# Linear attention with a GEGLU gate: the residual's x goes to another place, and the order of all engines is planned anew

## The chip, the cores and the metric

The kernel runs on one core of a Trainium2 chip. The metric is the time of one execution on the device in microseconds (us), the median of several runs.

## What is computed

```python
x = A_x                                   # [1, 2048, 512]
xn = layernorm(x)
qkv = xn @ wqkv                           # 32 heads of 16
phi = lambda t: where(t > 0, t + 1, exp(t)) + 1e-6
pq, pk = phi(q), phi(k)
kv = einsum("bhsd,bhse->bhde", pk, v);  z = pk summed over s
o = (pq @ kv) / (pq . z + 1e-6)           # by head
s = o @ wo
g = silu((gelu(xn @ w_gate) * (xn @ w_up)) @ w_down)   # hidden size 1792
out = x + s * g
```

## The kernel before

All data are float32. A matrix product is made of three matmuls on rounded halves: `split` (L494) writes a tile as a high part h (cast on ACT, L486) and a low part l = tile - h (subtraction on DVE, L492), and `sum3` (L498) adds h*h, h*l and l*h into one PSUM tile; the matmuls themselves are L508. On top of that, each 2x2 block product is made of seven products of sums of blocks instead of eight (`PRODUCTS`); X, Y, Z in the names of PSUM tiles are the accumulators of such a group, and the "forms" of an operand are the sums of its blocks that the seven products need, split into h and l.

The tokens are in two halves of 1024: p=1 is the second half, p=0 the first. The stages follow one another, with work of neighbouring stages mixed:

- first stage: layer norm, k, q, and the sum over the tokens; q and the forms of xn go to DRAM (q_d, x_d),
- the FFN of p=1, then of p=0: `quad` (PSUM tiles FX, FY, FZ; then fu and fe, copies of them that ACT makes; g and h on ACT, DVE and POOL) and `down` (DX, DY, DZ, added into acc by DVE, L1099),
- mixed into the FFN of p=0, the queries: a tile q comes back from q_d, POOL makes u = q * zacc, DVE den, its reciprocal rr and q * rr, PE transposes it (ptq, L1165), ACT copies it to pT, and it goes to DRAM (pn_d); `kv_part` loads the tiles wvg0 to wvg3 and PE makes pkv (L1245); `m_part` and its forms ms,
- the last stage, by `s_quad`: its operand's blocks pb come from pn_d and are made into forms, for p=1 in the place Xh and Xl (where the FFN's forms of xn were), for p=0 in sf0 and sf1. The products go to SX, SY, SZ, SV. With the gate g (for p=1 read back from DRAM as g1_0 to g1_7, for p=0 in acc) they are multiplied and added to x, which `x_again` loads once more from in_xt, one tile of 128 x 1024 for each k of 0 to 3: xp10 to xp13 for p=1, xp00 to xp03 for p=0. The sums go to out_y: for p=1 in four stores of 512 KB, for p=0 in nine smaller ones. The su2, su3 and se tiles are copies of SX that ACT makes, since the next product goes into the same SX.

Nothing of this is issued as written. Each operation is recorded by `do` of the class `Plan`, which knows for each its engine, its cost and what it has to wait for; PE's order is partly given by `pe_keys`, and `order` then finds one order for all five engines. `first_order` links the operations with lags (`MARGIN` is added to the lags into PE, into the other engines, and behind a load), schedules them by due times, and then, for each seed in `STEPS`, `nudged` shifts some of the due times at random in one place of the program and the schedule is made again. `MOVES` holds for each kind of DMA the time from issue to transfer, the time behind the transfer, and what is added to it for the engines. All DMAs are issued by SP, in the order found; a DMA whose wait is not over holds up those behind it. The engines, too, do their operations strictly in order.

A place holds one tile after another (`tile_in`): what writes the new tile waits for all readers of the tile before. The tiles xp and pb of the last stage rotate through the nine places of `ring("br", BR)`:

```python
got[k] = tile_in("dp", ring("br", BR), [P, HALF], F32, f"xp{p}{k}", 4)
dma(got[k], ext(xt[k * P:(k + 1) * P, p * HALF:(p + 1) * HALF]), 512, "first")
```

Of the kernel before, what the change touches and what calls it, by code (L numbers as in the profile page):

```python
# [11 lines left out]
F32 = mybir.dt.float32  # L12
# [5 lines left out]
P = 128  # L18
# [61 lines left out]
class Plan:  # L80

    RATE = 400.0
    MOVES = {"load": (0.72, 0.8, 0.0), "first": (0.72, 0.8, 0.7), "store": (0.45, 0.43, 0.0), "pieces": (0.45, 0.43, 0.6)}
    TAIL = {"PE": 0.19, "ACT": 0.13, "DVE": 0.12, "POOL": 0.07, "SP": 0.0}
    HEAD = {"PE": 0.14, "ACT": 0.01, "DVE": 0.01, "POOL": 0.04, "SP": 0.05}
    SAME = {"ACT": 0.15, "DVE": 0.13, "POOL": 0.09}
    BEGIN = 0.65
    ISSUE = 0.85
    ROUNDS = 14
    MARGIN = (0.1, 0.12, 1.0)  # L90
    STEPS = (28, 30, 51, 59, 73, 79, 109, 133, 151, 156, 172, 196, 242, 268, 273, 283, 305, 321, 344, 349, 369, 373, 379, 396, 407, 410, 416, 442, 471, 488, 517, 546, 586, 603, 690, 731, 752, 755, 789, 806, 811, 885, 999, 1028, 1071, 1082, 1197, 1229, 1260, 1313, 1328, 1454, 1461, 1487, 1505, 1523, 1531, 1582, 1598, 1619, 1714, 1744, 1809, 1825, 1884, 1908, 2199, 2256, 2425, 2509, 2559, 2587, 2830, 2905, 3004, 3279, 3386, 3411, 3415, 3433, 3457, 3592, 3702, 3921, 4000, 4006, 4030, 4174, 4182, 4277, 4425, 4583, 4716, 5136, 5149, 5175, 5225, 5401)
    WAIT = 0.3
    FIXED = 4

# [4 lines left out]
    def do(self, eng, cost, fn, out, *ins, more=(), key=None, name="", kb=0, kind="load"):  # L99
# [7 lines left out]
        op.pre, op.suc = set(), []  # L107
        op.way, op.land, gap = self.MOVES[kind]
        op.kb = kb / self.RATE + gap if kb else 0.0
# [204 lines left out]
    def first_order(self, pe_keys):  # L314

        self.link(pe_keys, 0.0, 0.0, 0.0)
        self.plain = self.ahead
        chain = self.link(pe_keys, *self.MARGIN)
        self.wide = self.ahead
# [25 lines left out]
    def order(self, pe_keys):  # L345

        late, done = self.first_order(pe_keys)
        at = self.plan_times(done)
        for seed in self.STEPS:
            late = self.nudged(late, at, seed)  # L350
# [27 lines left out]
def kernel(  # L378
# [17 lines left out]
    KT = D // P  # L396
# [16 lines left out]
    def tile_in(pool_name, unit, shape, dtype, name, parts=1):  # L413

        gen = gens[pool_name, unit] = Gen(gens.get((pool_name, unit)))
        kept = []

        def get():
            if not kept:
                kept.append(pools[pool_name].tile(shape, dtype, name=name, tag=f"{pool_name}{unit}", bufs=1))  # L420
            return kept[0]
        return View([Res() for _ in range(parts)], get, gen, pool_name == "ps")
# [3 lines left out]
    def ring(tag, places):  # L426
        n = count[tag] = count.get(tag, -1) + 1
        return places[n % len(places)]
# [28 lines left out]
    def ext(ap):  # L457
        return View((), lambda: ap)

    def dma(dst, src, kb, kind="load"):  # L460
        do("SP", 0.475, lambda o, i: nc.sync.dma_start(o, i), dst, src, kb=kb, kind=kind, name=kind)
# [857 lines left out]
    BR = [12, 13, 14, 6, 7, 8, 9, 10, 11]  # L1319
    HALF = 2 * NC  # L1320
# [87 lines left out]
    def x_again(p):  # L1408

        got = {}  # L1410
        for k in (0, 2, 1, 3):
            got[k] = tile_in("dp", ring("br", BR), [P, HALF], F32, f"xp{p}{k}", 4)
            dma(got[k], ext(xt[k * P:(k + 1) * P, p * HALF:(p + 1) * HALF]), 512, "first")
        return got

    forms, gg, xps = {}, {}, {}
    for p in (1, 0):
        forms[p] = s_forms(p)
        if p:
            gg[p] = {}  # L1420
            for n, key in enumerate(KEYS):
                gg[p][key] = U("fc" if n < 4 else "fg", FC if n < 4 else FG, f"g1_{n}")
                dma(gg[p][key], g1_d(n, n), 256)
            silus([gg[p][key] for key in KC])
        else:
            gg[p] = {key: acc[0, key] for key in KEYS}
        xps[p] = x_again(p)
        for c in range(2):
            s_quad(p, c, forms[p], gg[p], xps[p])
# [57 lines left out]
```

## Time and profile before

| | |
|---|---|
| median of 3 runs | 612.13 us (611.35 to 613.45) |
| profiled execution | 613.6 us, its span 611.9 us |
| busy PE / DVE / POOL / ACT | 595.7 / 482.1 / 361.6 / 337.8 us |
| granted clock of PE, mean | 0.993 |
| moved by DMA | 145.24 MB, 237 GB/s over the span |

The time is the whole execution, the span reaches from the first to the last instruction that the profiler has; 1.7 us lie around it. Busy times overlap, so they don't add up to the span. Three operations stand for most of what an engine does: a matmul of 128 x 512 (0.39 us from its start to its modelled end, though the next one starts 0.22 to 0.23 us later), an addition on DVE (0.68 us) and a copy or cast on ACT (0.59 to 0.62 us).

### The profile page before, as it was taken

How to read it: one execution, taken by the hardware profiler on the slowest of the kernel's cores; microseconds unless marked ns; L12 is line 12 of the kernel's file. 1: busy time of each engine (PE TensorE's matmuls, PEld its weight loads, DVE VectorE, ACT ScalarE, POOL GpSimd, SP SyncE). 2: the span in 40 equal slices, each digit the busy share in tenths (PEclk: the TensorE clock that was granted, in tenths of full speed). 3: DMA queues.
4: the chain of work that ended last, by engine and by line, in shares of the span. 5: the costliest groups of instructions: out<-in, count | busy, mean ns of one | idle time of the engine just before them, and what ended most of it. 6: DMA issues, size and time to landing. Idle time of an engine off the chain costs nothing. (4 is left out here: it accounts for less than half of the span.)

```text
span 611.9 us, 8235 instructions
## 1 busy us (share of the span) xinstructions
PE 595.7 (97%) x2696; PEld 491.0 (80%) x2696; DVE 482.1 (79%) x698; ACT 337.8 (55%) x611; POOL 361.6 (59%) x300
## 2 busy tenths in 40 slices
PE   8999999999999999999999999999999999989993
PEld 7888888888788888888888888886887888868883
DVE  6989988885798888998888837557557976959995
ACT  6677777875676644663563136453244532558731
POOL 4734754644778877886686126454226751758574
PEclk9999999999999999999999999999999999989998
DMA  7269521359558649764659975987499996788446
GB/s 260 75 225 300 182 76 71 121 172 328 204 202 302 252 151 334 283 221 143 227 220 407 363 299 189 300 284 276 140 319 325 313 346 210 273 293 278 152 139 238
DMA packets 59370, 145.24 MB, mean 237 GB/s; under 512 B 5568, under 2 KB 17088, under 8 KB 59328
## 3 DMA queue, kind: packets, MB, share of 16 engines
q1 hardware_dynamic: 59328, 144.73, 67.8%
q8 instruction: 21, 0.34, 0.2%
q14 instruction: 21, 0.17, 0.1%
HBM read 82.05 MB, written 62.65 MB: 236 GB/s over the span
## 5 line engine op out<-in xcount | busy, mean ns | idle before, releaser
L508 PE MATMUL FX<-Xh,w 128*128 128x512 f32 x448 | 151.7, 391 | 2.4 <-ACT fu L486 2.4
L508 PEld LDWEIGHTS FX<-Xh,w 128*128 128x128 f32 x448 | 83.8, 188 | 20.3 <-ACT fu L486 3.2
L1073 POOL TENSOR_TENSOR h<-h,g 128x512 f32<-128x512 f32 x42 | 61.5, 1468 | 64.3 <-DVE h L492 62.8
L492 POOL TENSOR_TENSOR h<-h,h 128x512 f32<-128x512 f32 x56 | 85.9, 1534 | 15.3 <-DVE hf2l L492 5.0
L508 PE MATMUL FX<-Xl,w 128*128 128x512 f32 x224 | 87.7, 392 | 0.0
L508 PE MATMUL FZ<-Xh,w 128*128 128x512 f32 x224 | 78.8, 393 | 0.0
L486 ACT COPY fu<-FX 128x512 f32<-128x512 f32 x56 | 32.9, 587 | 65.8 <-PE FX L508 57.0
L508 PE MATMUL gps<-pks,xns 128*128 128x512 f32 x192 | 52.4, 393 | 0.1
L508 PEld LDWEIGHTS FZ<-Xh,w 128*128 128x128 f32 x224 | 42.4, 190 | 9.2 <-DVE g L492 0.4
L508 PEld LDWEIGHTS FX<-Xl,w 128*128 128x128 f32 x224 | 42.2, 188 | 9.0 <-issue 0.2
L492 POOL TENSOR_TENSOR u<-q,zacc 128x512 f32<-128x512 f32 x16 | 22.5, 1427 | 42.7 <-DMA q<-q_d 21.4
L508 PE MATMUL FZ<-Xl,w 128*128 128x512 f32 x112 | 44.1, 393 | 0.0
L1099 DVE TENSOR_TENSOR acc<-acc,DX 128x512 f32<-128x512 f32 x48 | 32.5, 684 | 14.1 <-PE DX L508 13.8
L508 PEld LDWEIGHTS gps<-pks,xns 128*128 128x128 f32 x192 | 35.8, 188 | 7.5 <-PE fill L530 0.2
L1065 ACT ACTIVATE g<-g 128x512 f32<-128x512 f32 x42 | 26.6, 633 | 27.6 <-DVE g L492 27.5
L753 POOL TENSOR_TENSOR zacc<-zacc,kp 128x512 f32<-128x512 f32 x16 | 23.8, 1489 | 28.8 <-DVE kp L742 24.4
L508 PE MATMUL FY<-Xh,w 128*128 128x512 f32 x112 | 39.2, 391 | 0.0
L492 DVE TENSOR_TENSOR h<-fu,FZ 128x512 f32<-128x512 f32 x28 | 19.1, 684 | 22.6 <-ACT fu L486 13.1
L508 PE MATMUL X<-kq,Xh 128*128 128x512 f32 x96 | 31.8, 395 | 0.0
L492 DVE TENSOR_TENSOR g<-fu,FZ 128x512 f32<-128x512 f32 x28 | 19.1, 682 | 13.3 <-PE FZ L508 7.2
L1099 DVE TENSOR_TENSOR acc<-acc,DZ 128x512 f32<-128x512 f32 x32 | 21.9, 684 | 7.0 <-PE DZ L508 6.4
L486 ACT COPY fe<-FX 128x512 f32<-128x512 f32 x28 | 16.4, 587 | 18.2 <-PE FX L508 17.7
(423 smaller groups left out, 1610.8 us busy)
## 6 DMA issues: line engine op xcount, KB each, us to landing
w_d<-w SPq DMA_DIRECT2D x36, 512.0 KB, 5.2
w<-w_d SPq DMA_DIRECT2D x36, 512.0 KB, 5.3
wd_d<-wd SPq DMA_DIRECT2D x21, 512.0 KB, 4.9
wd<-wd_d SPq DMA_DIRECT2D x21, 512.0 KB, 4.9
x<-in_first SPq DMA_DIRECT2D x16, 256.0 KB, 3.3
q_d<-qp SPq DMA_DIRECT2D x16, 256.0 KB, 2.3
q<-q_d SPq DMA_DIRECT2D x16, 256.0 KB, 4.4
pn_d<-pT SPq DMA_DIRECT2D x8, 512.0 KB, 5.6
```

Of the source, the lines that this page charges most:

```text
L486: do("ACT", act(n), lambda o, i: nc.scalar.copy(o, i), dst, src, name=name)
L492: do(eng, c, lambda o, p, q: getattr(e, f"tensor_{op}")(o, p, q), dst, a, b, name=name)
L508: nc.tensor.matmul(o, v[i], v[i + 1], start=start and part == 0 and i == 0, stop=stop and part == 1 and i == len(v) - 2, skip_group_check=on)
L753: do("POOL", pool(D), lambda o, i: nc.gpsimd.tensor_add(o, o, i), zacc, p0, name="zacc")
L1065: curved("gelu", do("ACT", curve(NC), lambda o, i: nc.scalar.activation(o, i, AF.Gelu_apprx_tanh), g, ps if e is None else g, name="gelu"))
L1073: do("POOL", pool(NC), lambda o, i: nc.gpsimd.tensor_mul(o, o, i), h, g, name="h")
L1099: do("DVE", dve(NC), lambda o, i: nc.vector.tensor_add(o, o, i), a, ps, name="acc")
```

## The change

`x_again` takes for p=0 one whole tile of 128 x 4 x 1024 in the place "h" of the pool xf, where Xh was, the high parts of the forms of the last stage's p=1; it gives a quarter of it to each k. Before, the loads of xp00 to xp03 waited for a store of p=1 to leave a place of the ring; now they wait for the last reader of Xh. In `MOVES` the third number of "load" and "store" is 0.15 instead of 0, and `MARGIN` is larger. `STEPS` holds other seeds, 84 instead of 98. Both programs have the same operations, DMAs and transfers; the edits to the tables move them on every engine.

```diff
-    MOVES = {"load": (0.72, 0.8, 0.0), "first": (0.72, 0.8, 0.7), "store": (0.45, 0.43, 0.0), "pieces": (0.45, 0.43, 0.6)}
+    MOVES = {"load": (0.72, 0.8, 0.15), "first": (0.72, 0.8, 0.7), "store": (0.45, 0.43, 0.15), "pieces": (0.45, 0.43, 0.6)}
...
-    MARGIN = (0.1, 0.12, 1.0)
-    STEPS = (28, 30, 51, 59, 73, 79, 109, 133, 151, 156, 172, 196,
...
+    MARGIN = (0.2, 0.2, 3.0)
+    STEPS = (12, 17, 30, 37, 54, 58, 64, 68, 88, 91, 95, 112, 120,
...
     def x_again(p):
 
         got = {}
+        if not p:
+            whole = tile_in("xf", "h", [P, KT, HALF], F32, "xp0", 0)
         for k in (0, 2, 1, 3):
-            got[k] = tile_in("dp", ring("br", BR), [P, HALF], F32, f"xp{p}{k}", 4)
+            got[k] = tile_in("dp", ring("br", BR), [P, HALF], F32, f"xp{p}{k}", 4) if p else whole.part(
+                [Res() for _ in range(4)], (slice(None), k))
             dma(got[k], ext(xt[k * P:(k + 1) * P, p * HALF:(p + 1) * HALF]), 512, "first")
         return got
```

How the order moves is shown at three places. The last number of a name is a running number of the tile; it differs between the two programs and means nothing here.

**Where the last stage begins** (in the profile before, 530 to 545 us). pb100 and pb101 are operands of the last stage, g1_4 a part of the gate, ms00 to ms12 the other operand, pn1_d and g1_d tiles in DRAM. SP before:

```order
L461 DMA pb101_5131<-pn1_d_85 128x512 x2
L461 DMA ms10_5163<-m10_d_168 128x1024
L461 DMA g1_4_5222<-g1_d_86 128x512
L461 DMA ms03_5186<-m03_d_167 128x1024
L461 DMA pb100_5196<-pn1_d_85 128x512 x2
L461 DMA ms01_5216<-m01_d_165 128x512
L461 DMA ms12_5248<-m12_d_170 128x1024
```

and now:

```order
L461 DMA ms00_5109<-m00_d_164 128x1024
L461 DMA pb101_5126<-pn1_d_85 128x512 x2
L461 DMA ms02_5140<-m02_d_166 128x1024
L461 DMA ms03_5169<-m03_d_167 128x1024
L461 DMA ms10_5175<-m10_d_168 128x1024
L461 DMA pb100_5201<-pn1_d_85 128x512 x2
L461 DMA g1_4_5220<-g1_d_86 128x512
L461 DMA ms01_5230<-m01_d_165 128x512
```

The two loads of pb100 stood behind those of g1_4 and ms03, and stand ahead of g1_4 now. ACT before:

```order
L1065 ACTIVATE g21_0_5231<-FX0_5032 128x512
L486 CAST Xh0_255<-pb100_5196 128x512
L486 COPY fu3_1_5239<-FX1_5136 128x512
L486 COPY pT6_5246<-ptq6_5176 128x4x128
L486 COPY pT6_5246<-ptq7_5177 128x4x128
L486 CAST Xh0_255<-pb100_5196 128x512
L486 CAST hf0h_5218<-h21_1_5269 128x512
```

and now:

```order
L486 CAST Xh0_247<-pb101_5126 128x512
L486 CAST hf0h_5222<-h11_1_5184 128x512
L486 COPY fu3_1_5225<-FX1_5135 128x512
L486 CAST Xh0_247<-pb101_5126 128x512
L486 COPY pT6_5203<-ptq7_5187 128x4x128
L1065 ACTIVATE g21_0_5243<-FX0_5007 128x512
L1065 ACTIVATE g12_0_5171<-g12_0_5171 128x512
L486 CAST Xh0_247<-pb100_5201 128x512
L486 CAST hf0h_5222<-h21_1_5262 128x512
```

The copy fu3_1 from PSUM stood behind the first cast of pb100; now it stands ahead of all of them, and behind a cast of pb101.

**The queries' tile q0** (460 to 467 us in the profile before). PE transposes it into ptq0 and ptq1. PE before:

```order
L508 MATMUL FX4_4494<-Xh0_255,w42_4361 128x512 x2
L508 MATMUL FX4_4494<-Xl0_268,w42_4361 128x512
L508 MATMUL FX4_4494<-Xh0_255,w42_4361 128x512
L508 MATMUL FX4_4494<-Xl0_268,w42_4361 128x512
L508 MATMUL FX4_4494<-Xh0_255,w42_4361 128x512
L508 MATMUL FZ4_4558<-Xh0_255,w42_4361 128x512 x2
L508 MATMUL FZ4_4558<-Xl0_268,w42_4361 128x512
L508 MATMUL FZ4_4558<-Xh0_255,w42_4361 128x512
L508 MATMUL FZ4_4558<-Xl0_268,w42_4361 128x512
L508 MATMUL FZ4_4558<-Xh0_255,w42_4361 128x512
L1165 MATMUL ptq0_4568<-ident_174,q0_4473 128x128 x4
L1165 MATMUL ptq1_4569<-ident_174,q0_4473 128x128 x4
```

and now:

```order
L508 MATMUL FY5_4588<-Xh0_247,w50_4434 128x512 x2
L508 MATMUL FY5_4588<-Xl0_266,w50_4434 128x512
L508 MATMUL FY5_4588<-Xh0_247,w50_4434 128x512
L508 MATMUL FY5_4588<-Xl0_266,w50_4434 128x512
L508 MATMUL FY5_4588<-Xh0_247,w50_4434 128x512
L508 MATMUL FZ4_4550<-Xh0_247,w43_4409 128x512 x2
L508 MATMUL FZ4_4550<-Xl0_266,w43_4409 128x512
L508 MATMUL FZ4_4550<-Xh0_247,w43_4409 128x512
L508 MATMUL FZ4_4550<-Xl0_266,w43_4409 128x512
L508 MATMUL FZ4_4550<-Xh0_247,w43_4409 128x512
L1165 MATMUL ptq0_4613<-ident_174,q0_4479 128x128 x4
L1165 MATMUL ptq1_4614<-ident_174,q0_4479 128x128 x4
```

Before, ptq0 followed the products of w42 for FX4 and FZ4; now those of w43 for FX4 and FZ4 and those of w50 for FX5 and FY5 have come ahead of it. Between the transposes of the tile before (ptq14 and ptq15) and these stand 46 products of 512 columns before and 66 now. In the same way, from the reading of wvg0 to that of wvg3 PE has 18 products of 512 columns before and 24 now.

**The end.** SP before, from the load of xp00 on:

```order
L461 DMA xp00_5527<-in_xt 128x1024
L461 DMA out_y<-xp10_5398 128x1024
L461 DMA out_y<-xp12_5450 128x1024
L461 DMA xp02_5698<-in_xt 128x1024
L461 DMA xp01_5676<-in_xt 128x1024
L461 DMA out_y<-xp11_5311 128x1024
L461 DMA xp03_5736<-in_xt 128x1024
L461 DMA out_y<-xp13_5373 128x1024
L461 DMA out_y<-xp01_5676 128x512
```

and now:

```order
L461 DMA out_y<-xp12_5449 128x1024
L461 DMA out_y<-xp10_5398 128x1024
L461 DMA xp0_5649<-in_xt 128x1024 x4
L461 DMA out_y<-xp11_5308 128x1024
L461 DMA out_y<-xp13_5356 128x1024
L461 DMA out_y<-xp0_5649 128x512 x7
```

The four loads of x for p=0 (xp0 is the whole tile) now stand together, behind the stores of xp12 and xp10; before, they stood between stores. On POOL, the addition that completes xp10 is now the last of a row:

```order
L492 TENSOR_TENSOR xp11_5308<-xp11_5308,g1_2_5412 128x512
L492 TENSOR_TENSOR pb001_5483<-pb001_5483,pb000_5427 128x512
L492 TENSOR_TENSOR pb011_5516<-pb011_5516,pb010_5460 128x512
L492 TENSOR_TENSOR pb011_5516<-pb011_5516 128x512
L492 TENSOR_TENSOR pb001_5483<-pb001_5483 128x512
L492 TENSOR_TENSOR xp10_5398<-xp10_5398,g1_1_5379 128x512
L492 TENSOR_TENSOR acc0_2_3724<-acc0_2_3724,se1_3_5681 128x512
```

Before, it stood further ahead there:

```order
L492 TENSOR_TENSOR g1_2_5419<-g1_2_5419,se1_1_5535 128x512
L492 TENSOR_TENSOR pb001_5479<-pb001_5479 128x512
L492 TENSOR_TENSOR xp10_5398<-xp10_5398,g1_1_5386 128x512
L492 TENSOR_TENSOR pb011_5519<-pb011_5519 128x512
L492 TENSOR_TENSOR xp11_5311<-xp11_5311,g1_2_5419 128x512
```

It moved behind the four operations on pb that make forms for p=0. And DVE, where the first row that touches xp0 is the addition of SY2, for k=0, which is SP's third of the four loads. Now:

```order
L492 TENSOR_TENSOR SY2_5596<-acc0_0_3707,SY2_5596 128x512
L492 TENSOR_TENSOR acc0_5_3797<-acc0_5_3797,SV2_5728 128x512
L492 TENSOR_TENSOR xp0_5649<-xp0_5649,SY2_5596 128x512
L492 TENSOR_TENSOR SZ2_5664<-su2_2_5694,SZ2_5664 128x512
L492 TENSOR_TENSOR acc0_1_3776<-acc0_1_3776,SZ2_5664 128x512
L492 TENSOR_TENSOR acc0_4_3810<-acc0_4_3810,SX2_5608 128x512
L492 TENSOR_TENSOR SZ3_5707<-su2_3_5755,SZ3_5707 128x512
L492 TENSOR_TENSOR SZ3_5707<-acc0_3_3783,SZ3_5707 128x512
L492 TENSOR_TENSOR xp0_5649<-xp0_5649,SZ3_5707 128x512
```

Before:

```order
L492 TENSOR_TENSOR acc0_5_3823<-acc0_5_3823,SV2_5718 128x512
L492 TENSOR_TENSOR SZ2_5661<-su2_2_5664,SZ2_5661 128x512
L492 TENSOR_TENSOR acc0_1_3798<-acc0_1_3798,SZ2_5661 128x512
L492 TENSOR_TENSOR SY2_5620<-acc0_0_3781,SY2_5620 128x512
L492 TENSOR_TENSOR acc0_4_3844<-acc0_4_3844,SX2_5608 128x512
L492 TENSOR_TENSOR xp00_5527<-xp00_5527,SY2_5620 128x512
```

The addition into x moved ahead of the one that makes SZ2 from su2.

More of the change, by code (lines that the diff above doesn't have):

```diff
@@ L89 @@
     ROUNDS = 14
-    MARGIN = (0.1, 0.12, 1.0)
-    STEPS = (28, 30, 51, 59, 73, 79, 109, 133, 151, 156, 172, 196, 242, 268, 273, 283, 305, 321, 344, 349, 369, 373, 379, 396, 407, 410, 416, 442, 471, 488, 517, 546, 586, 603, 690, 731, 752, 755, 789, 806, 811, 885, 999, 1028, 1071, 1082, 1197, 1229, 1260, 1313, 1328, 1454, 1461, 1487, 1505, 1523, 1531, 1582, 1598, 1619, 1714, 1744, 1809, 1825, 1884, 1908, 2199, 2256, 2425, 2509, 2559, 2587, 2830, 2905, 3004, 3279, 3386, 3411, 3415, 3433, 3457, 3592, 3702, 3921, 4000, 4006, 4030, 4174, 4182, 4277, 4425, 4583, 4716, 5136, 5149, 5175, 5225, 5401)
+    MARGIN = (0.2, 0.2, 3.0)
+    STEPS = (12, 17, 30, 37, 54, 58, 64, 68, 88, 91, 95, 112, 120, 130, 135, 178, 219, 243, 254, 272, 291, 296, 307, 334, 350, 358, 391, 399, 421, 482, 518, 595, 713, 745, 884, 952, 1037, 1318, 1332, 1383, 1390, 1412, 1459, 1532, 1540, 1563, 1676, 1910, 1984, 2062, 2080, 2109, 2148, 2154, 2161, 2184, 2185, 2285, 2316, 2343, 2539, 2627, 2682, 2732, 2736, 2755, 2779, 2791, 2797, 2850, 2885, 3006, 3525, 3544, 3782, 3810, 3819, 4355, 4555, 4804, 4809, 5047, 5174, 5351)
     WAIT = 0.3
```

## The prediction

> **What bounds the kernel now.** I read the page's busy times first, then PE's waits, then stretches of the span, then the timelines around each wait.
>
> ```profile
> PE 595.7 (97%) x2696; PEld 491.0 (80%) x2696; DVE 482.1 (79%) x698; ACT 337.8 (55%) x611; POOL 361.6 (59%) x300
> ```
>
> PE is busy for 97% of the span, and the change takes no matmul away, so it can gain only what PE idles, what the clock loses, and what follows PE's last product. The waits of PE, with total, count and longest in us:
>
> ```profile
> core 0 of [0], span 611.9 us
> PE FX L508 <- ACT fu L486: 2.4, 1, 2.4
> PE ptq L1165 <- DVE q L1158: 1.5, 1, 1.5
> PE warm L530 <- DVE ones L519: 1.1, 1, 1.1
> PE pkv L1245 <- DMA wvg<-g_d: 0.8, 1, 0.8
> PE k L508 <- DVE Xl L492: 0.6, 1, 0.6
> PE k L508 <- ACT Xh L486: 0.3, 1, 0.3
> PE pt L677 <- DVE xn L655: 0.2, 1, 0.2
> ```
>
> Only seven waits, 6.9 us. The reader sees that each of the large ones is one event, so the question is whether the new order has that event. The same profile by stretches (busy us and count of each engine, then granted clock, DMA share, GB/s):
>
> ```profile
> core 0: us, PE busy (x) PEld busy (x) DVE busy (x) ACT busy (x) POOL busy (x), PEclk, DMA share, GB/s
> 311.00:326.00 15.00, 15.00 (x68) 12.43 (x67) 14.33 (x17) 8.54 (x16) 11.34 (x9) 1.00 0.93 355
> ...
> 540.00:560.00 20.00, 18.76 (x76) 15.37 (x77) 15.52 (x20) 14.65 (x26) 16.72 (x12) 0.91 0.87 294
> 560.00:580.00 20.00, 20.00 (x89) 16.32 (x88) 19.83 (x31) 15.96 (x30) 11.15 (x8) 1.00 0.59 193
> ...
> 541.20:546.00 4.80, 4.76 (x14) 3.79 (x15) 2.12 (x4) 2.72 (x5) 4.09 (x3) 0.64 0.72 239
> ```
>
> A full stretch holds 89 matmuls in 20 us, 0.225 us each. In 541 to 546 the clock averages 0.64: at half clock that is 4.8 x 0.36 / 0.5 = 3.5 us, which cost 1.7 us. It follows the 2.4 us wait; the 1.5 us wait had no such dip.
>
> **The wait at 541 (-4.1).** On PE, ACT, SP and POOL, in this order:
>
> ```profile
> 538.47 0.39 PE L508 MATMUL DX<-hf1h,wd 128*128 128x512 f32 x1
> 541.24 0.74 PE L508 MATMUL FX<-Xh,w 128*128 128x512 f32 x2 [2.38 <-ACT fu L486]
> ...
> 542.06 0.60 PE L508 MATMUL FX<-Xh,w 128*128 128x512 f32 x1
> ...
> 540.08 0.62 ACT L486 CAST Xh<-pb 128x512 fp32r<-128x512 f32 x1 [3.34 <-DMA pb<-pn_d]
> 540.61 0.58 ACT L486 COPY fu<-FX 128x512 f32<-128x512 f32 x1
> ...
> 534.78 0.32 SPq L461 DMA_DIRECT2D g<-g_d  x1
> 535.68 0.84 SPq L461 DMA_DIRECT2D pb<-pn_d  x2
> ...
> 533.45 1.30 POOL L1073 TENSOR_TENSOR h<-h,g 128x512 f32<-128x512 f32 x1
> ...
> DMA to landing us min/median/max: 4.4/4.8/5.1
> ```
>
> ACT takes its work in order. Its copy fu, for which PE waits, stood behind a cast of pb, which waited 3.34 us for pb's loads (the last line: those two, 4.4 and 5.1 us). They were issued late because SP takes its DMAs in order too, and stood at g's load until POOL had finished h at 534.75. In the new order both queues differ: SP issues the two loads of pb100 ahead of g1_4, and ACT does fu3_1 ahead of every cast of pb100. Ahead of it now stands a cast of pb101, whose loads stand four rows ahead of these in the queue. So 2.4 us of idling and 1.7 us of half clock go. Next late is hf0h, which ACT casts behind pb100: by the distance in PE's new order (products times 0.225) about 1.2 us to spare. If pb100 landed over 1.2 us late, the wait would be back there. The moves past g1_4 and ms03 cost those DMAs at most the issue of two others (0.84 us), and ACT reads g1_4 only behind its last cast of pb100.
>
> The Trainium skill, "TensorE: Matmul & The Clock Gate" (Part 1, What's actually happening), states that the clock falls to half after an idle window of about 3.4 us, in a free-running window of 3413 ns. By it the gap of 2.38 us need not have cost any clock, and this term would be -2.4, and the sum -2.55. The trace agrees with the length (3.5 us at half clock) and not with the threshold, since a gap of 2.38 us was enough here; I go by the trace.
>
> **The wait at 466 (-1.5).** SP, its landing, POOL, DVE:
>
> ```profile
> 454.52 0.88 SPq L461 DMA_DIRECT2D q<-q_d  x2
> DMA to landing us min/median/max: 4.2/4.8/5.4
> ...
> 460.47 2.54 POOL L492 TENSOR_TENSOR u<-q,zacc 128x512 f32<-128x512 f32 x2 [5.24 <-DMA q<-q_d]
> ...
> 464.97 1.29 DVE L1158 SCALAR_TENSOR_TENSOR q<-q,rr 128x512 f32<-128x512 f32 x2
> ```
>
> The query tile has one buffer, so the loads start when PE has transposed the tile before it, and load, POOL's products and DVE's norm run in a row until 466.26: about 12 us, whatever the order. PE had 46 products between the two groups of ptq, 10.3 us, and ran dry. The new order has 66, 14.9 us: 20 x 0.225 = 4.5 us more against a wait of 1.5. It goes, with 3 us to spare. The other gaps between such groups are at least 13 us.
>
> **The wait at 414 (-0.75).** The last two loads of wvg, their landings, and PE:
>
> ```profile
> 408.53 0.37 SPq L461 DMA_DIRECT2D wvg<-in_first  x1
> ...
> DMA to landing us min/median/max: 5.5/5.6/5.7
> ...
> 414.79 1.13 PE L1245 MATMUL pkv<-wvg 128*128 128x128 f32 x8 [0.76 <-DMA wvg<-g_d]
> ```
>
> The slot comes free when PE has read wvg0. From there to wvg3 PE had 18 products of 512 columns, and now has 24: 1.35 us more against 0.76. I take it as gone, with 0.6 us to spare; loads that take 6.3 us instead of 5.7 would bring some of it back.
>
> **The start (-0.5).** The waits for Xl, Xh and xn at 8 to 14 us (1.1 us together) meet another order of the first loads; 0 and -1.1 are the ends, I take the middle. The wait for ones at the very start stays.
>
> **New waits inside (+0.6, +0.5).** In the down products of the second half, near 540 us, PE now returns to the PSUM tile DZ010 after only two other products, and DVE must take the old sum out in between (first row; the second is DVE's end of waiting after the stop at 541):
>
> ```profile
> L1099 DVE TENSOR_TENSOR acc<-acc,DZ 128x512 f32<-128x512 f32 x32 | 21.9, 684 | 7.0 <-PE DZ L508 6.4
> ...
> 546.13 0.69 DVE L492 TENSOR_TENSOR h<-fu,FZ 128x512 f32<-128x512 f32 x1 [1.89 <-PE FZ L508]
> ```
>
> A product of 0.39 us and this addition make 1.07 us, where three steps of PE are 0.67: 0.4 us, and 0.6 with the two hand-overs. Nothing hides it, as PE has no other work in its queue. The rest of the order I can't read to the tenth: waits like the small ones above (0.2 to 0.8 us) may be anywhere, so 0 to 2, and I take 0.5. DVE, 19.83 of 20 us busy from 560 on, is the likeliest place. That PE comes 4 us earlier does not make that worse: DVE idled for PE in that wait as well, and it begins its unbroken run with PE's products at 546.
>
> **The end (+1.5, from -1.0 to +7).** SP at the end, the landings of the two loads issued at 590.79 and 592.09, those of the five earlier loads of x, then POOL, PE, and the last three stores:
>
> ```profile
> 590.79 1.64 SPq L461 DMA_DIRECT2D xp<-in_xt  x2
> DMA to landing us min/median/max: 3.5/4.8/6.1
> ...
> DMA to landing us min/median/max: 4.5/5.0/5.2
> ...
> 589.87 1.83 POOL L492 TENSOR_TENSOR xp<-xp,g 128x512 f32<-128x512 f32 x1
> 598.35 5.47 POOL L492 TENSOR_TENSOR xp<-xp,acc 128x512 f32<-128x512 f32 x4 [2.12 <-DMA xp<-in_xt]
> ...
> 602.33 0.28 PE L508 MATMUL SX<-sf1h,ms 128*128 128x256 f32 x1
> ...
> L461 SPq DMA_DIRECT2D out_y<-xp x3: 451/510/541, 605.9 to 607.0; - x3
> DMA to landing us min/median/max: 3.8/4.1/4.3
> ```
>
> Before, three loads of x had to wait until a store of the other half had landed; POOL waited 2.1 us for one, off PE's path. PE ended at 602.6 and the last store landed at 607.0 + 3.8 = 610.8, 8.2 us behind it. The change takes the wait for landings away, but puts all four loads into SP's queue behind the store of xp10, and that one behind POOL's addition to xp10, now the last of POOL's for p=1. Before, the last of these (then to xp11) ended at 591.7, 10.9 us ahead of PE's end, and POOL has the same operations ahead of it. So all four start there; their place is free by then, as PE's last reading of Xh is several us earlier in its order. The first takes 5.0 us. The next follow at 1.5 us each at best (512 KB at the 355 GB/s of the stretch at 311), at 3.9 at worst (the two loads above landed at 594.3 and 598.2). The third, xp00, lands 8.0 to 12.8 us after the start: from 2.9 us ahead of PE's end to 1.9 behind it.
>
> It is needed earlier. DVE's addition into xp00 now stands ahead of DVE's SZ2, whose PSUM operand su2 frees the buffer for ACT's next copy, and PE waits for that before its last products. From the load's landing I count: two additions on DVE 1.4, a copy on ACT 0.6, PE's six products 1.4, a second copy of the same tile, which nothing covers now, 0.9, twelve half products 1.4, hand-overs 0.8; then PE's drain, additions by halves and the store's landing (4.1) 5.7: 12.2 us. With the third load 2.9 us ahead of PE's end, the last store lands 9.3 us behind where PE would have ended, against 8.2: +1.1. PE then idles about 3 us, which may halve the clock for its last products: at most 1.4 more, so I take +1.5. If the loads are in time, POOL's and DVE's waits at the end go: -1.0. At 3.9 us a load it is 1.9 + 12.2 - 8.2 = +5.9, with the half clock about +7.
>
> **The sum.** -4.1 - 1.5 - 0.75 - 0.5 + 0.6 + 0.5 + 1.5 = -4.25. The profiled execution took 613.6 us (span 611.9), so 609.35 by its own measure. It lies 1.5 us above the median, 612.13, close to what the half clock cost; if the median runs had no half clock, they gain 1.7 less. From 612.13: 607.9 with it, 609.6 without. I take 608.5.
>
> **Rivals.**
> - *The loads of x come too late (the other side).* All four loads behind POOL's addition, 3.9 us apart. For it: two of them did land so in this trace, and here four stand together with stores. Against it: the five earlier loads took 5.0 us alone. It turns slower by 0.3% when the end costs 7.6 us instead of 1.5, thus when xp00 lands 13 to 14.5 us after the start of the four, with or without the half clock. At +7 the profiled measure is 614.9, the median about 613.7; landings 2 us apart give 610.5. Chance 0.18.
> - *ACT or DVE brings the wait at 541 back*, with pb100 late by more than the 1.2 us to spare. For it: one row's wait of 3.34 us did that here. Against: SP no longer waits for POOL ahead of it. The 4.1 us stay: 612. Chance 0.14.
> - *A wait of over 2.4 us at a new place*, since every queue's order is new, costs its length and 1.7 us of clock. It gives 612.6 with one, 616 with two. For it: one load late by 3 us did so. Against: the order keeps all transfers and products, and I found none. Chance 0.15.
> - *The half clock at 542 did not come from the gap* and stays: 608.5 + 1.7 = 610.2. Against: PE's steps stretch from 542.06 on (0.60 us for a product), 0.8 us after the gap, and the 1.5 us gap, without it, is the shorter one. Chance 0.06. The threshold of the Trainium skill, quoted with the wait at 541, would have it so.
> - *Forecast, stalls gone and the end between -1 and +2.5*: 605 to 610. Chance 0.47.
>
> **The numbers.** 0.3%, 1.84 us, is about what a measurement can tell from no change: faster ends at 610.3, slower begins at 614.0. Faster: 0.47, of the loads 0.03, of 541 0.04, of the new place 0.07, of the clock 0.03, together 0.64. Slower: the loads 0.06, 541 0.04, the new place 0.06: 0.16. The rest, 0.20, is the same. The range is 604.5 (all four waits gone, none new, loads in time) to 613.2 (loads 3 us apart, or one wait back). The forecast's own range is 605 to 610.
>
> **What would show it.** PE's waits: FX for fu, ptq for q and pkv for wvg absent, and the clock 1.00 in 540 to 560. A wait of PE for DVE's acc at about 535, near 0.6 us. At the end SP issuing four loads of x in a row, right behind the stores of xp12 and xp10, and DVE's xp waiting for the third, with PE's SX waiting for ACT's copy. Wrong it would be if PE's list shows another single wait over 2 us, or if DVE waits over 5 us for x.

## The result, and the profile after

The changed kernel takes 606.38 us in the median of 5 runs (604.86 to 608.48), the kernel before 612.28 us (611.35 to 613.83): a ratio of 0.9899, with a 95% interval from 0.9871 to 0.9927. The forecast was 608.5 us, in a range from 604.5 to 613.2. The profiled execution took 605.75 us with a span of 604.0, 7.9 us less than the span before; the medians lie 5.9 us apart, and 7.5 us in the second measurement of the changed kernel (below). The page's busy times:

```profile
PE 593.9 (98%) x2696; PEld 490.7 (81%) x2696; DVE 471.4 (78%) x698; ACT 334.8 (55%) x611; POOL 357.1 (59%) x300
```

PE's waits (total, count, longest in us):

```profile
PE SX L508 <- ACT su L486: 2.7, 2, 2.0
PE warm L530 <- DVE ones L519: 1.1, 1, 1.1
PE k L508 <- DVE Xl L492: 0.9, 1, 0.9
PE DZ L508 <- DVE acc L1099: 0.3, 1, 0.3
```

The waits for fu, for q and for wvg are gone from the list. The wait for DVE's acc is there, and the largest is a new one, at the end. By stretches (busy us and count, clock, DMA share, GB/s):

```profile
400.00:420.00 20.00, 20.00 (x100) 15.88 (x98) 11.38 (x15) 9.12 (x16) 11.60 (x12) 1.00 0.87 306
460.00:480.00 20.00, 20.00 (x94) 16.66 (x93) 16.21 (x24) 12.14 (x24) 14.38 (x12) 1.00 0.89 311
540.00:560.00 20.00, 19.67 (x86) 15.72 (x85) 18.41 (x25) 13.41 (x25) 15.45 (x11) 1.00 0.88 302
580.00:600.00 20.00, 16.41 (x70) 12.96 (x68) 15.58 (x26) 4.04 (x7) 9.37 (x7) 0.88 0.77 262
```

PE is at full clock in all three places where it stood before, and full there but for the 0.33 us at DZ010. It idles in the last stretch. There, the timelines of SP, DVE and PE:

```profile
581.72 0.34 SPq L461 DMA_DIRECT2D out_y<-xp  x1
582.17 3.07 SPq L461 DMA_DIRECT2D xp<-in_xt  x4
...
591.79 0.69 DVE L492 TENSOR_TENSOR xp<-xp,SY 128x512 f32<-128x512 f32 x1 [2.84 <-DMA xp<-in_xt]
...
593.75 0.50 PE L508 MATMUL SX<-sf0h,ms 128*128 128x512 f32 x1 [2.02 <-ACT su L486]
596.23 0.58 PE L508 MATMUL SX<-sf0h,ms 128*128 128x256 f32 x1 [0.73 <-ACT su L486]
```

The time from issue to landing, of the four loads and then of the last three stores:

```profile
DMA to landing us min/median/max: 5.6/8.1/9.0
...
L461 SPq DMA_DIRECT2D out_y<-xp x3: 332/332/333, 599.2 to 601.0; - x3
DMA to landing us min/median/max: 1.9/2.0/2.0
```

The four loads go out behind the store of xp10, DVE waits 2.84 us for the third of them, and PE waits for the copy that hangs on DVE. But the last stores land in 2.0 us, where they took 3.8 to 4.3 before.

To see where the 7.9 us come from, I laid the matmuls of both traces side by side by the work done and read the lag between them: -1.5 us by 390 us (of it -0.95 in the first 20), -1.2 at wvg, -1.8 at q0, -4.25 at fu, +0.8 at DZ010, +4.5 at PE's two waits for su with the half clock behind them, and -4.4 behind PE's last product (the last store lands 3.8 us behind it, 8.2 before). The sum is -7.85.

### The profile page after: what moved, and what is told of

It is laid out like the page before. It is cut to its first block, busy times and chain, and to the rows that moved or that the text cites. A ratio compares the mean times of both kernels' runs of the same rounds, so it can differ in the third digit from the quotient of the medians.

```text
span 604.0 us, 8229 instructions
## 1 busy us (share of the span) xinstructions
PE 593.9 (98%) x2696; PEld 490.7 (81%) x2696; DVE 471.4 (78%) x698; ACT 334.8 (55%) x611; POOL 357.1 (59%) x300
## 4 chain that ended last, share of the span: by engine, by line
PE 95%; DMA 2%; DVE 1%; ACT 0%; SPq 0%; issue 0%; DVEq 0%; ACTq 0%
PE FX L508 25%; PE FZ L508 13%; PE DX L508 13%; PE gps L508 7%; PE DZ L508 6%; PE FY L508 6%; PE X L508 5%; PE DY L508 3%; PE SX L508 3%; PE Z L508 3%; PE q L508 2%; PE k L508 2%; DMA xp<-in_xt 1%; PE Y L508 1%; PE ptq L1165 1%; PE pt L677 1%
## 5 line engine op out<-in xcount | busy, mean ns | idle before, releaser
L1073 POOL TENSOR_TENSOR h<-h,g 128x512 f32<-128x512 f32 x42 | 63.1, 1508 | 69.9 <-DVE h L492 65.2
L492 POOL TENSOR_TENSOR h<-h,h 128x512 f32<-128x512 f32 x56 | 83.7, 1494 | 17.8 <-DVE hf5l L492 4.4
```

The costliest lines, as they stand in the source:

```text
L492: do(eng, c, lambda o, p, q: getattr(e, f"tensor_{op}")(o, p, q), dst, a, b, name=name)
L1073: do("POOL", pool(NC), lambda o, i: nc.gpsimd.tensor_mul(o, o, i), h, g, name="h")
```

## The experiments

The theory after the result: the gain is three stops of PE that the new order has not, the largest one made by SP's queue; the end is a loss on PE and a gain in the stores. The rivals: the half clock was not the stop's doing; the place of xp0 made the gain; any order by the new tables would do.

**SP in the plan's order, kernel before.** The description of the kernel before says that SP issues the DMAs in the plan's order. That is wrong: the plan hands its order to four engines only, and the DMAs are put in order once more when the program is built. One line changes that:

```diff
-ENGINES = {mybir.EngineType.PE, mybir.EngineType.Activation, mybir.EngineType.DVE, mybir.EngineType.Pool}
+ENGINES = {mybir.EngineType.PE, mybir.EngineType.Activation, mybir.EngineType.DVE, mybir.EngineType.Pool, mybir.EngineType.SP}
```

> The kernel before with one edit: SP is added to the engines whose order is the plan's own, so that the DMAs are issued as planned. In the program of before the order of SP was made once more behind the plan, and only there did the load of g1_4 come ahead of those of pb100. Theory A (SP's head-of-line wait for g1_4 made the stop at 541, and the stop made the half clock): PE's wait for fu goes, the clock is 1.00 in 540 to 560, the time falls by about 4.3 us (2.4 idle, 0.3 of overlap lost at a restart, 1.7 clock), to about 608 from 612.3. Rival (the half clock is not due to the stop): the clock still dips near 542 and the time falls by 2.6. Rival (pb100 is late anyway, for PE's or DVE's sake): ACT still waits over 2 us for pb and the time stays within 1 us.

607.77 us (607.32 to 608.73), ratio 0.9906 (0.9887 to 0.9925) to before's 613.79 on that chip. SP and ACT around the place in that kernel's timeline:

```profile
534.07 0.79 SPq L461 DMA_DIRECT2D pb<-pn_d  x2
536.80 0.38 SPq L461 DMA_DIRECT2D g<-g_d  x1
...
538.61 0.62 ACT L486 CAST Xh<-pb 128x512 fp32r<-128x512 f32 x1 [0.98 <-DMA pb<-pn_d]
539.14 0.58 ACT L486 COPY fu<-FX 128x512 f32<-128x512 f32 x1
```

The same stretch as above:

```profile
540.00:560.00 20.00, 20.00 (x89) 16.53 (x89) 17.31 (x24) 15.62 (x28) 18.54 (x12) 1.00 0.94 325
```

pb's loads go out 2.7 us ahead of g's, ACT waits 0.98 us instead of 3.34, and PE does not stop. Theory A holds. PE's order is the same in both programs, so their products can be compared one by one: just ahead of the stop PE is 0.9 us later than before (it lost 1.1 us at the start, where it waits longer for Xh), and behind the half clock 3.1 us earlier. The stop was worth 4.0 us. The last store also lands 6.4 us behind PE's last product instead of 8.2: by the names in the traces, at least 7 of the 348 DMAs stand in another place, some of them at the end. These 3.1 and 1.8 are the 4.9 us between the two profiled executions; the medians lie 6.0 apart, and the last 1 us is not explained.

**ACT's cast moved alone, kernel before.** Here and below, behind(n, m) moves operation n directly behind operation m in the plan's list, ahead of the issuing.

```diff
+    behind(2841, 2718)    # the first cast of pb100, behind the copy fu3_1
```

> The kernel before, SP as it was, with one operation moved: ACT's first cast of pb100 stands behind the copy fu3_1 instead of ahead of it. pb's loads stay late. Theory A (two queues in series make the stop, so either is enough): PE's wait at 541 falls from 2.4 us to under 0.5, no half clock, 3.5 to 4.3 us faster. Rival (the late pb100 is what counts): the wait comes back within a few us at the next operation on ACT or DVE behind pb100, of 1.5 us or more, and the gain is under 2 us.

613.56 us (611.02 to 616.24), ratio 0.9996 (0.9973 to 1.0019): nothing won in the median. PE's timeline:

```profile
541.99 0.49 PE L508 MATMUL DX<-hf1h,wd 128*128 128x512 f32 x1 [1.89 <-ACT pT L486]
542.94 0.73 PE L508 MATMUL FZ<-Xh,w 128*128 128x512 f32 x2 [0.46 <-DVE h L492]
```

The stop moved to the next thing on ACT behind the cast, the copy pT, 0.8 us later, and with the wait for h it is as long as before (1.89 + 0.46 against 2.38). No half clock followed it in this profile, one of the two shortest executions of twelve (611.31). My theory of two queues of which either is enough is wrong: with the load as late as it was, the moved cast only moved the place where PE stopped.

**PE made to idle twelve times, changed kernel.**

```diff
+    again = {831: 4, 990: 5, 1107: 6, 1294: 7, 1411: 8, 1598: 9, 1889: 4, 2023: 5, 2129: 6, 2322: 7, 2445: 8, 2607: 9}
-        o.fn()
+        for _ in range(again.get(o.n, 1)):
+            o.fn()
```

> The changed kernel with twelve of ACT's copies fu done 4, 5, 6, 7, 8 and 9 times over (two of each, 25 us or more apart), which only adds time: PE then idles at twelve places by different lengths, about 1 to 4 us. It tells what idle time of PE the clock answers to. Theory A (any idle time of somewhat over 2 us halves the clock for 3.4 us): all gaps above about 2.2 us are followed by half clock, none below 1.5. Rival (a rule of a free-running window of 3.4 us that must be idle as a whole): only gaps over 3.4 us are followed by it, and the one of 2.4 us was something else. Third (a window of 3.4 us that asks for a share of busy time): between some 1.5 and 3.4 us some gaps are followed by it and others of the same length are not.

652.07 us, one execution, which is used for its clock alone. PE's twelve waits for fu were 0.7 to 3.9 us long. The six of 2.3, 3.1, 3.2, 3.3, 3.65, 3.85 us and one of 3.9 were followed by half clock; those of 0.7, 1.1, 1.2, 1.3 and 1.4 were not. A stop at the end, 1.92 us for su, was followed by it too (at 636 to 643 below). The clock changed only at times 3.413 us or a multiple of it apart. So I cut the traces at those times (PE's busy us is the first number with a count; the clock is the third number from the end). This kernel, and then before, at the stop of 1.5 us and at that of 2.4:

```profile
206.18:209.60 3.42, 1.46 (x6) 1.24 (x7) 0.95 (x2) 3.33 (x7) 3.34 (x5) 1.00 0.91 299
209.60:213.01 3.41, 3.41 (x9) 2.63 (x8) 2.75 (x3) 1.98 (x6) 2.18 (x2) 0.50 0.18 71
213.01:216.42 3.41, 3.41 (x16) 2.82 (x15) 1.14 (x2) 2.12 (x5) 0.48 (x1) 1.00 0.38 154
...
636.26:639.68 3.42, 1.50 (x7) 0.94 (x6) 2.35 (x4) 0.59 (x1) 1.36 (x2) 1.00 1.03 419
639.68:643.09 3.41, 2.68 (x8) 1.67 (x7) 2.75 (x5) 0.59 (x1) 2.23 (x2) 0.50 0.89 343
```

```profile
463.56:466.97 3.41, 1.92 (x12) 1.38 (x11) 3.31 (x7) 0.79 (x3) 0.70 (x1) 1.00 0.88 321
466.97:470.39 3.42, 3.42 (x19) 2.78 (x17) 2.60 (x3) 2.59 (x6) 3.24 (x2) 1.00 0.98 348
538.66:542.07 3.41, 1.03 (x5) 0.69 (x5) 1.34 (x3) 1.99 (x4) 0.51 (x1) 1.00 0.92 339
542.07:545.48 3.41, 3.41 (x10) 2.67 (x9) 1.25 (x2) 1.85 (x4) 3.41 (x3) 0.50 0.64 194
```

A window in which PE was busy for 1.50 us or less is followed by one at half clock; after 1.92 it was not. That is the third theory, a share of busy time; the twelve waits alone would fit theory A as well. The kernel with the place alone (below) tells them apart: its PE stopped for 2.95 us at 542.81, longer than before, and the clock stayed up:

```profile
537.63:541.05 3.42, 2.23 (x10) 1.50 (x8) 1.36 (x3) 0.13 (x1) 0.00 (x0) 1.00 0.94 333
541.05:544.46 3.41, 1.65 (x7) 1.39 (x8) 1.89 (x3) 2.08 (x4) 1.33 (x1) 1.00 0.67 252
544.46:547.87 3.41, 3.41 (x17) 2.82 (x16) 2.46 (x4) 2.34 (x4) 3.41 (x4) 1.00 0.84 233
```

A boundary cut that stop into 1.2 and 1.8 us, and neither window fell to 1.5 us of work. By theory A the clock would have fallen. The rule of the Trainium skill cited in the prediction ("TensorE: Matmul & The Clock Gate", Part 1) has the right window, 3413 ns and free-running, but the runs did not need a whole idle window: somewhat over half of one was enough.

**The changed kernel again, and with SP in the plan's order.**

> The changed kernel once more, unaltered, so that the variants of it have it on the same chip. Both theories: about 0.99 of before (606 to 608).

606.18 us (605.72 to 606.46), ratio 0.9876 (0.9849 to 0.9903), beside the two repairs and the place alone (below). With the line for SP:

> The changed kernel with the same one edit: SP in the plan's own order. At the end, the four loads of x for the first half then stand ahead of the store of xp10 and no longer wait for POOL's addition; they can start when PE has read Xh for the last time, about 3.5 us earlier. Theory A (the third of these loads sets the end): DVE's wait of 2.8 us for x goes, PE's wait of 2.0 us for su goes with it, and the clock stays up in PE's last products; PE's other wait of 0.7 us, for the copy between the last two groups, stays; 2 to 3.5 us faster, about 603.5 from 606.4. Rival (DVE, POOL and the stores bound the end anyway): PE's wait goes, but the end moves by less than 1 us. Rival (the earlier loads run into the pb loads and share the bandwidth): the third load still lands after 590 and the gain is under 1 us.

603.32 us (602.83 to 604.15), ratio 0.9833 (0.9812 to 0.9854) to before's 613.79, timed beside the kernel before with SP's order. SP and DVE in its timeline:

```profile
578.15 1.89 SPq L461 DMA_DIRECT2D xp<-in_xt  x4
...
589.30 0.68 DVE L492 TENSOR_TENSOR xp<-xp,SY 128x512 f32<-128x512 f32 x1
```

And the one line for su in PE's waits:

```profile
PE SX L508 <- ACT su L486: 0.7, 1, 0.7
```

The loads go out 4.0 us earlier, DVE does not wait, PE's 2.0 us is gone and the 0.7 stays. Theory A holds: the third load set PE's end, and its place in SP's queue cost 2.6 us by the two ratios (in the profiles PE ends 3.2 us earlier, and gets ahead only where that wait was). This version is faster than both kernels, and none of those below beats it.

**Two repairs on PE, with SP in the plan's order.** One product into DZ010 four places later, and then also the last products into SZ3 between the two groups into SX3:

```diff
+    behind(2801, 2901)
+    behind(3064, 3057)    # the second kernel only
+    behind(3065, 3064)    # DVE's use of SZ3, likewise
```

> The changed kernel with SP in the plan's order, and with the first product of the third group into DZ010 moved four products later on PE (behind those into SX1 and SX0), so that DVE's addition has 0.9 us more. Theory A (PE waits there for the PSUM tile alone): PE's wait for acc, 0.33 us, goes, and 0.5 to 0.8 us with the lost overlap, against SP's order alone. Rival (the products moved ahead wait instead, for the new Xh): the wait turns up at SX1 and the time stays within 0.3 us.

603.57 us (602.79 to 603.78), ratio 0.9832 (0.9805 to 0.9859), as with SP's order alone. The wait at DZ010 went, but this profile has one of 0.66 us for acc at 503.8 that the others have not. What the repair is worth stays open; it is under 0.5 us in the median.

> As the one with DZ010, and at the end the last four products into SZ3 stand between the two last groups into SX3 (0.9 us of work for PE while ACT copies SX3 out), with DVE's use of SZ3 behind them. Theory A (PE's 0.73 us there is on the path that sets the end): PE's wait for su falls under 0.2 and the time falls by 0.5 to 1.0 us more. Rival (DVE's last additions bound the end, and SZ3 now comes later): no gain, 0 to 0.8 us slower than with DZ010 alone.

604.78 us (604.05 to 605.8), ratio 0.9855 (0.9827 to 0.9883), 1.2 slower than with DZ010 alone. The rival holds, and by more than its 0.8: PE's wait is gone and PE ends 0.9 us earlier than in the profile with DZ010 alone (which had the wait at 503.8), but DVE's use of SZ3 comes later, and the last store lands 6.05 us behind PE instead of 4.0. Moved work of PE does not mend this wait; what the wait costs by itself is not shown.

**The place alone, in the order of before.**

```diff
             got[k] = tile_in("dp", ring("br", BR), [P, HALF], F32, f"xp{p}{k}", 4)
+            if not p and k:
+                got[k].get = lambda k=k: whole()[:, k]    # a quarter of a tile in the place of Xh
```

> The kernel before, its tables and the order of PE, DVE, ACT and POOL unaltered, with the place alone changed: xp01, xp02 and xp03 go to the place of Xh (xp00 keeps its place, since it is loaded before Xh's last reading there). It tells what the place is worth by itself. Theory A (the waits for landed stores lay off the path): the loads of x are issued 1.8 to 10 us earlier, POOL's waits for them (2.1 and 0.4 us) go, the time falls by 0 to 0.5 us. Rival (they set the end): 1.5 to 2.5 us faster. The 541 stop is as in before in both.

611.32 us (609.73 to 613.1), ratio 0.9964 (0.9946 to 0.9982): 2.4 us. The rival holds. PE's three stops are there, longer than before (3.0, 2.0, 0.8 us), but without the half clock, and so PE ends as before by luck (602.5). DVE ends 0.5 us later (606.1). What is shorter is the issue and the landing of the last stores: the very last goes out 0.1 us behind DVE's last addition instead of 1.4, and the last eight land in 2.0 to 4.0 us:

```profile
L461 SPq DMA_DIRECT2D out_y<-xp x8: 332/332/425, 599.0 to 606.2; - x8
DMA to landing us min/median/max: 2.0/2.7/4.0
```

Before, the ten stores issued between 599.9 and 607.0 stood behind the load that had waited for a store to land, went out in a bunch and took 3.8 to 5.9 us each. The waits of SP for landed stores, which theory A put beside the path, were on it by way of the last stores.

**Does it add up?** SP's order, and the transposes of q0 (with ACT's copies and the DMAs that hang on them) 12 products later on PE; then the place as well:

```diff
+    behind(2411, 2440)
+    for n, m in ((2412, 2411), (2413, 2412), (2482, 2413), (2483, 2482), (2414, 2483)):
+        behind(n, m)
```

> The kernel before with SP in the plan's order (607.8 alone), and with the transposes ptq0 and ptq1, ACT's copies of them and the DMAs that wait for them moved behind 12 further products of PE (2.7 us). Theory A (the wait at 466 is worth its idle time and a restart): PE's wait for q, 0.9 us in that kernel's profile, goes, and the time falls by 1.0 to 1.5 us, to 606.5. Rival (the next tile's chain, which now starts 2.7 us later, makes the next transposes wait): the wait comes back at ptq2, gain under 0.5.

609.99 us (609.0 to 612.58), ratio 0.9953 (0.9932 to 0.9973), thus 2 to 3 us slower than SP's order alone (607.77, and 0.9906). PE's wait for q is gone, but a new one is there:

```profile
PE FX L508 <- ACT fu L486: 1.9, 1, 1.9
```

Neither theory had this. ACT's copies of ptq0 moved with it, and a copy fu stands behind them. PE also waits 0.6 us for DVE's g and 0.5 for su. Moving one step of the chain is not enough, and what the stop at 466 costs by itself stays unshown.

> As the one with the moved transposes, and with xp01, xp02 and xp03 in the place of Xh. Theory A (the parts add up): 2.4 us less, as the place alone gave, about 604.1, and with it nearly all of the difference between the two kernels is made by three moves in the old order. Rival (SP's order already had put a store ahead and won part of the end): 0.5 to 1.5 us less, about 605.5.

609.84 us (609.09 to 612.76), ratio 0.9947 (0.9923 to 0.9972). The place brings 0.15 us here, inside the scatter; neither theory had that. The last four stores landed in 2.0 us without the place already, and the last one 5.7 us behind PE in both. The parts do not add up: place and SP's order seem to mend the same end.

**The planner's parts.** The old tables with the new place, and the new tables with the old place (each plan made anew, so that most rows move):

> The kernel before with the change to x_again alone: the tables stay, but the plan is made anew, and nearly every row of the order differs, since the list of seeds was found for another program. Theory A (the seeds fit one program only, the place is worth 2.4 us, and the stops fall by chance): between 609 and 616, with at least one PE wait of over 1 us that before did not have. Rival (the parts add up, and the tables do their work for any program): 611.3, the same three stops as before.

616.24 us (612.55 to 617.3), ratio 1.0046 (1.0021 to 1.0071): slower by 0.5%, with a wait of 2.4 us where the kernel before had one of 0.8:

```profile
PE pkv L1245 <- DMA wvg<-g_d: 2.7, 2, 2.4
```

That is theory A, though the median is just above its range. The last store lands 4.0 us behind PE, so the end is mended here too; PE ends 4.4 us later than before.

> The changed kernel without the change to x_again: new margins and new seeds, x of the first half in the ring again. Theory A (as above): between 606 and 614, with at least one PE wait of over 1 us that the changed kernel does not have, and at the end the loads of x wait for landed stores again. Rival (the parts add up): 606.2 + 2.4 = 608.6 and no stop in the middle, since wider margins keep PE away from landings.

608.51 us (607.63 to 609.96), ratio 0.9923 (0.9892 to 0.9953), as the rival had it. No wait over 1.1 us; the longest in the middle is 0.9:

```profile
PE warm L530 <- DVE ones L519: 1.1, 1, 1.1
PE SX L508 <- ACT su L486: 1.0, 2, 0.7
PE DZ L508 <- DVE hf0l L492: 0.9, 1, 0.9
```

At its end the loads of x wait for landed stores again, and still the last store lands 4.1 us behind PE; in the changed kernel's two profiles it is 3.8 and 4.1. So the new tables, too, shorten this end, without the place. The 2.3 us to the changed kernel's 606.18 (2.9 by the ratios) lie in PE, which ends at 601.5 instead of 599.3.

The seeds by themselves don't carry over: the old ones, with the new place, got a new stop of 2.4 us. With the new tables, the kernel without the place has no such stop either. Whether the wider margins do that, or the seeds' luck, one kernel can't tell, and margins alone were not tried.

## Why the prediction was right or wrong

The time came out 2.1 us below the forecast's 608.5, inside its range, and most of the mechanism as put. In detail, by the profiled runs:

- *The three stops* were read rightly, and they are most of the gain. Each was worth 0.15 to 0.45 us more than put: -4.25, -1.8 and -1.2 against -4.1, -1.5 and -0.75. A restart adds 0.27 us to the idle time: the next product would have started 0.16 us ahead of the last one's end, and the first after a stop is followed by another after 0.34 us instead of 0.23. For the largest stop an experiment gives 4.0; the other two are read from the traces alone.
- *What made the stop at 541* was the head of SP's queue, as put: the kernel before with SP's order alone loses the stop, and with ACT's cast moved alone it does not. But I took SP's queue for a work of the tables. It is made behind the plan, where the plan had g1_4's load behind pb100's already.
- *The half clock* came from the stop, as put, in the profiled run. That it goes with every such stop is wrong: it hangs on where the 3.413 us windows fall, and one of 2.95 us passed without it. The half clock here was in part chance. It may also be why before scatters (610.6 to 618.3 us in the 31 runs beside the last four kernels), where before with SP's order ran from 607.3 to 608.7 in five. That is not shown: one trace of before is kept, and the old tables with the new place scatter by 4.8 us at a mean clock of 0.995 or more.
- *The wait at DZ010* came, but at 546.8 and not about 535: 0.33 us of idling and the restart make the 0.6 that were put, and 0.8 were lost in that stretch.
- *The third load of x* landed 3.0 us ahead of where PE would have ended, and 2.9 had been put. That it agrees to a tenth is luck: the load took 9.5 us from the start of the four and not 8.0, but the four began 12.5 us ahead of that end and not 10.9. Behind the first load and a gap of 2.6 us they landed 1.3 us apart, not 3.9, so the slower rival had no ground. PE lost 4.5 us with the half clock, between the 3.6 of the count without it and the 5.0 with all of it; the sum had taken little of the half clock (0.4 of 1.4).
- *The step that failed* is the sum behind it: "PE's drain, additions by halves and the store's landing (4.1) 5.7". It was 3.8, as the stores landed in 2.0 us. The landing in the trace of before was not the price of a store but that of a bunch, which the change itself dissolved. With that, the end is +0.1 instead of +1.5. The prediction also called POOL's wait of 2.1 us, for a load held up by landing stores, off PE's path; it was, but the same hold-up delayed the last stores.
- *Smaller terms*: the start and all up to 390 us gave -1.5 for -0.5, and the allowance of +0.5 for unknown waits was not needed. With the end (1.4) and the three stops (0.9), less the 0.2 at DZ010, these make the 3.6 us between the predicted -4.25 and -7.85 on the profiled runs. What made the -1.5 up to 390 us is not shown.
- *The rivals*: none came. By its letter the sign of being wrong did (another single wait over 2 us): PE's wait of 2.02 us for su. It is the wait that the prediction had put at the end, behind DVE's wait for the third load.

## What to carry to other kernels

When an engine stops behind a late load, look first at what stands ahead of that load in the DMA queue, and whether that queue's order is the one you planned; mending the waiting engine alone only moved the stop. A store's time to landing belongs to the queue around it, so when a change spreads out a bunch of stores, count them at what a lone one takes. An edit to a planner's tables is read best as a list of stops that the new order has or has not, and a stop's price here was its idle time, about 0.3 us for the restart, and sometimes half clock for 3.4 us.

## What the runs showed of the hardware

PE's clock changed in windows of 3.413 us, in a raster fixed within a profile: in all 14 profiles, each window at full clock with at most 1.50 us of PE work was followed by one at half clock (11 of them, up to PE's last product), and none with 1.58 us or more. Out of the half clock it takes more: a window with 2.3 us of work at half clock was followed by another. A stop of 1.92 us inside one window halved the clock, one of 2.95 us cut by a boundary did not. Stores of 256 KB and less landed in 1.9 to 2.0 us at the end of the changed kernel, issued 0.9 us apart, and in 3.8 to 5.9 us before, where ten stores went out within 7 us; in the changed kernel, too, the first three behind its loads and stores of 512 KB took 4.9 to 6.2 us.
